# Transposing one more group of attention probabilities on VectorE instead of TensorE

## The chip, the cores and the metric

The kernel runs on one core of one Trainium2 chip. The metric is the device time of one execution in microseconds; the program is launched once and does everything on the chip. A core has five engines with their own instruction streams: TensorE (PE) for matmuls, VectorE (DVE), ScalarE (ACT), GpSimd (POOL) and SyncE (SP), which here issues nearly all DMAs.

## The reference

Attention inside chunks of 64 tokens, and then a two-layer network with a squared ReLU. There are 8 x 576 = 4608 tokens, 8 heads of 64, and the network is 512 to 2048 to 512.

```
scores = scale * q_c @ k_c.T             # per chunk of 64 tokens, per head
attn = exp(scores - max); attn /= attn.sum + 1e-9
x = (attn @ v_c) as 4608 x 512
h = x @ w_in                             # 4608 x 2048
g = s * relu(h)**2 + b
out = g @ w_out                          # 4608 x 512
```

All inputs are float32, and the kernel keeps float32 accuracy in the large products by splitting each operand into a high and a low part and adding three matmuls: high by high, high by low, low by high.

## The kernel before

Tokens come in 36 tiles of 128, and four tiles make a block, so there are nine blocks. Within a block the loop over `j` runs over the 16 slices of the inner dimension 2048: `up(j)` multiplies x by one slice of `w_in` (12 matmuls of 128x512 into `ps_h`), `square(j)` and `bias(j)` turn the result into the two parts `gh` and `gl`, and `down(j - 2)` multiplies these by a slice of `w_out` (12 matmuls into the four `ps_o` tiles). `down` lags two steps behind, so the loop has 18 steps.

The attention of the next block is computed inside the loop of the present one, in two groups of two tiles. `attention_plan` holds a table of places: a place `(j, 0)` is before `up(j)`, `(j, 1)` behind it, and `(j, 2)` between `square(j)` and `bias(j)`. The first group starts at n = 1 and the second at n = 9. For the second group that gives: scores behind up(9), the maximum at (9, 2), the subtraction at (10, 2), exp at (11, 0), the sum at (11, 2), the division (`norm`) before up(13), the transposition of the probabilities, and the product with the values (`values`) behind up(15), whose result is split into the two parts of x (`x_hi` on ScalarE, `x_lo` on VectorE) in the steps 16.

The probabilities `p` are 128 rows (query tokens) by 8 sets of 128 columns. The product with the values needs them transposed, as `pT`. There are two ways in the code. `transposes` and `copies` have TensorE transpose each 128x128 set into the PSUM tile `ps_a` behind up(14) (line L203), and ScalarE copies them to SBUF before up(15) (L217). `turn` has VectorE transpose them from SBUF to SBUF, in 16 instructions that each handle the 32x32 blocks of one position in all 8 sets (L212): four of them between `square(13)` and `bias(13)`, six before up(14), six between `square(14)` and `bias(14)`. Groups of tiles from 8 on use `turn`.

The first block is special, since the weights are prepared in its loop. They arrive as 64-bit numbers and are turned to float32 and split into parts by the class `Pair`, step by step: `scale` and `tail` on ScalarE (L102, L106), `bits` on VectorE (L112, L114), `add` on GpSimd (L120), `hi` on ScalarE (L124), `lo` on VectorE (L128). Pair k holds the `w_in` slice of step k + 1 and the `w_out` slice of step k - 1. In step j VectorE makes `lo` of pair j, which the third matmul of up(j + 1) needs first, and the `bits` of pair j + 2. So up(15) needs the `lo` of pair 14, and down(14) that of pair 15.

The order on each engine is the order of the code; nothing is moved by a scheduler. `square(j)` is L273 on ScalarE and L274 on VectorE, `bias(j)` is L279 on ScalarE and L280 on VectorE, `up` is L266, `down` L291, the scores L172, `values` L225.

Of the kernel before, what the change touches and what calls it, by code (L numbers as in the profile page):

```python
# [19 lines left out]
def local_attention_then_squared_relu_mlp(ctx: ExitStack, tc, qkv, w, s, b, out):  # L20
# [221 lines left out]
    def block(tb0, bank):  # L242
        x = [xp.tile([P, NHP, 4 * P], F32R, name=n) for n in ("xh", "xl")]
        return x, [Attention(tb0 + i, x, i * P, bank) for i in range(0, 4, N)]
# [73 lines left out]
    def attention_plan(tb0):  # L318
        x, groups = block(tb0, steady_bank)
        plan = {}  # L320
        for a, n in zip(groups, (1, 9)):
            for at, *fs in (((n - 1, 0), a.load_qk, a.load_v), ((n, 1), a.scores), ((n, 2), a.peak), ((n + 1, 2), a.sub),
                            ((n + 2, 0), a.exp), ((n + 2, 2), a.sum), ((n + 4, 0), a.norm),
                            ((n + 6, 1), a.values), ((n + 7, 0), a.x_hi), ((n + 7, 2), a.x_lo)):
                plan.setdefault(at, []).extend(fs)

            if a.tb < 8:
                turns = ((n + 5, 1), a.transposes), ((n + 6, 0), a.copies)
            else:
                turns = [(at, partial(a.turn, range(*r))) for at, r in (((n + 4, 2), (0, 4)), ((n + 5, 0), (4, 10)), ((n + 5, 2), (10, 16)))]  # L330
            for at, f in turns:
                plan.setdefault(at, []).append(f)
        return x, plan, plan.pop((0, 0))
# [3 lines left out]
    for a in (one, two):  # L337
        a.p = wp.tile([P, 4, DM], F32, name="wp")[:, 0:2, :].rearrange("p i (g c k) -> p (i g) c k", g=NHP, c=2)
    next_x, plan, (load_next_qk, load_next_v) = attention_plan(4)
    pair = [Pair(k) for k in range(NJ)]  # L340
    one.load_qk()
# [61 lines left out]
    for tb0 in range(0, NTB, 4):  # L403
# [42 lines left out]
        if tb0 + 8 < NTB:  # L446
            next_x, plan, loads = attention_plan(tb0 + 8)
# [33 lines left out]
```

## Time and profile before

| | |
|---|---|
| median of 3 runs | 864.5 us (864.43 to 864.71) |
| profiled execution | 864.6 us, its span 862.8 us |
| granted TensorE clock | 1.000 |
| PE busy | 847.9 us (98%), 5874 matmuls |
| DVE busy | 472.2 us (55%) |
| ACT busy | 295.4 us (34%) |
| POOL busy | 42.1 us (5%) |

The time runs from the start to the end of one execution on the device; the span is from the first to the last instruction in the trace. In the rows shown below a matmul's duration overlaps that of the next one, since matmuls are pipelined; what a matmul costs is read from start to start. In a row of the timeline stand the start, the duration, the engine, the line, the operation, the tile written and those read, the shape and the count; a bracket at the end gives the idle time before it and what ended that. The rows of groups have busy time and mean duration in ns, then the idle time before. The rows of waits have the total, the number and the longest. The first block lasts from about 22 us to 124.7 us.

### The profile page before, as it was taken

How to read it: one execution, taken by the hardware profiler on the slowest of the kernel's cores; microseconds unless marked ns; L12 is line 12 of the kernel's file. 1: busy time of each engine (PE TensorE's matmuls, PEld its weight loads, DVE VectorE, ACT ScalarE, POOL GpSimd, SP SyncE). 2: the span in 40 equal slices, each digit the busy share in tenths (PEclk: the TensorE clock that was granted, in tenths of full speed). 3: DMA queues.
4: the chain of work that ended last, by engine and by line, in shares of the span. 5: the costliest groups of instructions: out<-in, count | busy, mean ns of one | idle time of the engine just before them, and what ended most of it. 6: DMA issues, size and time to landing. Idle time of an engine off the chain costs nothing.

```text
span 862.8 us, 13668 instructions
## 1 busy us (share of the span) xinstructions
PE 847.9 (98%) x5874; PEld 697.2 (81%) x5874; DVE 472.2 (55%) x710; ACT 295.4 (34%) x437; POOL 42.1 (5%) x24
## 2 busy tenths in 40 slices
PE   8899999999999999999999999999999999999998
PEld 7677788888888888888888888888888888888886
DVE  6898945646464646364554556473636464543222
ACT  5777743222322232223222332223222322232222
POOL 2434310000000000000000000000000000000000
PEclk9999999999999999999999999999999999999999
DMA  8646430200210030203020212002020300010001
GB/s 330 232 168 245 149 108 15 74 2 25 98 39 36 2 122 1 74 1 123 0 74 1 73 51 72 4 25 98 3 72 1 123 0 26 1 49 1 1 0 50
DMA packets 20369, 55.41 MB, mean 64 GB/s; under 512 B 2260, under 2 KB 2516, under 8 KB 20308
## 3 DMA queue, kind: packets, MB, share of 16 engines
q1 hardware_dynamic: 20160, 54.40, 18.0%
q8 instruction: 46, 0.75, 0.4%
q10 hardware_dynamic: 148, 0.13, 0.0%
q14 instruction: 15, 0.12, 0.0%
HBM read 45.09 MB, written 9.44 MB: 63 GB/s over the span
## 4 chain that ended last, share of the span: by engine, by line
PE 88%; DVE 7%; issue 2%; ACT 2%; DMA 1%; POOL 0%; SPq 0%; ACTq 0%; POOLq 0%
PE ps_o L291 42%; PE ps_h L266 41%; PE ps_a L225 2%; PE ps_a L172 2%; DVE wp L128 2%; DVE ps_h L274 1%; DVE f L114 1%; DVE f L112 1%; DVE g L280 1%; ACT g L279 1%; DMA raw<-in_w_dram 1%; DVE z L191 0%; PE ps_h L67 0%; DVE m L177 0%; POOL f L120 0%
## 5 line engine op out<-in xcount | busy, mean ns | idle before, releaser
L291 PE MATMUL ps_o<-wp,g 128*128 128x512 f32 x1728 | 415.6, 391 | 0.0
L266 PE MATMUL ps_h<-xh,wp 128*128 128x512 f32 (+1 forms) x1160 | 378.9, 389 | 5.6 <-DVE g L280 3.4
L291 PEld LDWEIGHTS ps_o<-wp,g 128*128 128x128 f32 x1728 | 322.3, 188 | 67.8
L274 DVE SCALAR_TENSOR_TENSOR ps_h<-ps_h,sb,r 128x512 f32<-128x512 f32 x144 | 109.2, 758 | 320.2 <-ACT r L273 319.7
L266 PEld LDWEIGHTS ps_h<-xh,wp 128*128 128x128 f32 x1160 | 216.8, 188 | 53.0 <-DVE wp L128 4.1
L266 PE MATMUL ps_h<-xl,wp 128*128 128x512 f32 (+1 forms) x580 | 224.9, 388 | 0.0
L273 ACT ACTIVATE r<-ps_h 128x512 f32<-128x512 f32 x144 | 85.9, 597 | 366.9 <-PE ps_h L266 366.9
L279 ACT ACTIVATE g<-ps_h,sb 128x512 fp32r<-128x512 f32 x144 | 99.1, 688 | 125.9 <-DVE ps_h L274 125.9
L280 DVE SCALAR_TENSOR_TENSOR g<-ps_h,sb,g 128x512 fp32r<-128x512 f32 x144 | 107.6, 747 | 47.8 <-ACT g L279 46.9
L266 PEld LDWEIGHTS ps_h<-xl,wp 128*128 128x128 f32 x580 | 108.9, 188 | 22.1
L212 DVE STREAM_TRANSPOSE pT<-p 32x256 f32<-32x256 f32 x224 | 97.5, 435 | 3.9
L120 POOL TENSOR_TENSOR f<-f,raw 128x1024 int32<-128x1024 int32 (+1 forms) x17 | 39.5, 2323 | 67.6 <-DVE f L114 48.7
L308 ACT COPY f<-ps_o 128x512 f32<-128x512 f32 (+1 forms) x35 | 20.4, 583 | 41.4 <-PE ps_o L291 39.2
L114 DVE SCALAR_TENSOR_TENSOR f<-raw,f 128x1024 uint32<-128x1024 uint32 (+1 forms) x17 | 21.9, 1286 | 0.5
L102 ACT ACTIVATE f<-raw 128x1024 f32<-128x1024 f32 (+1 forms) x17 | 18.5, 1088 | 10.4 <-DMA raw<-in_w_dram 9.2
L128 DVE TENSOR_TENSOR wp<-f,wp 128x1024 fp32r<-128x1024 f32 (+1 forms) x17 | 22.0, 1294 | 0.0
L240 DVE TENSOR_TENSOR xl<-ps_a,xh 128x512 fp32r<-128x512 f32 x32 | 20.5, 683 | 1.7 <-ACT xh L236 1.7
L196 DVE TENSOR_TENSOR p<-p,z 128x1024 f32<-128x1024 f32 x16 | 19.6, 1226 | 0.6
L172 PEld LDWEIGHTS ps_a<-raw 64*64 64x64 f32 x960 | 15.4, 134 | 5.3 <-issue 5.3
L225 PEld LDWEIGHTS ps_a<-pT,v 64*64 64x64 f32 x960 | 15.4, 134 | 5.3 <-issue 4.9
L124 ACT CAST wp<-f 128x1024 fp32r<-128x1024 f32 (+1 forms) x17 | 16.9, 996 | 7.6 <-POOL f L120 7.5
L177 DVE TENSOR_REDUCE m<-ps_a 128x16 f32<-128x1024 f32 x16 | 19.4, 1215 | 0.0
(45 smaller groups left out, 214.9 us busy)
## 6 DMA issues: line engine op xcount, KB each, us to landing
raw<-in_w_dram SPq DMA_DIRECT2D x32, 512.0 KB, 4.8
raw<-in_qkv_dram SPq DMA_DIRECT2D x30, 512.0 KB, 4.6
out_dram<-f SPq DMA_DIRECT2D x35, 256.0 KB, 2.1
v<-in_qkv_dram SPq DMA_DIRECT2D x30, 256.0 KB, 3.0
wp<-in_qkv_dram SPq DMA_DIRECT2D x6, 512.0 KB, 6.0
wp<-in_qkv_dram SPq DMA_DIRECT2D x6, 256.0 KB, 8.0
out_dram<-f ACTq DMA_DIRECT2D x1, 128.0 KB, 2.1
out_dram<-f SPq DMA_DIRECT2D x1, 128.0 KB, 2.0
```

The costliest lines, as they stand in the source:

```text
L114: nc.vector.scalar_tensor_tensor(out=u, in0=high, scalar=0x80000000, in1=u, op0=ALU.bitwise_and, op1=ALU.bitwise_or)
L120: nc.gpsimd.tensor_tensor(out=i, in0=i, in1=low.bitcast(I32), op=ALU.add)
L128: nc.vector.tensor_tensor(out=lo, in0=f, in1=hi.bitcast(F32), op=ALU.subtract)
L172: nc.tensor.matmul(out=self.ps[cols, c, i * NHP + hp, :], lhsT=qk[rows, 0, h, :], rhs=qk[rows, 1, h, :], start=True, stop=True)
L212: nc.vector.transpose(out=self.pT[k].rearrange("p i a t -> p (i a) t")[:, :, t], in_=p[t, :, k])
L225: nc.tensor.matmul(out=ps[i if apart else 0][cols, c, i * NHP + hp, :], lhsT=self.v[i][rows, h, :], rhs=self.pT[rows, i, hp, cols], start= ...
L266: nc.tensor.matmul(out=self.ps[j][:, cols], lhsT=w[:, c, :], rhs=x[:, c, :], start=(c == 0 and i == 0), stop=(c == NHP - 1 and i == 2))
L273: nc.scalar.activation(out=r, in_=ps, func=AF.Relu)
L274: nc.vector.scalar_tensor_tensor(out=ps, in0=ps, scalar=s_col, in1=r, op0=ALU.mult, op1=ALU.mult)
L279: nc.scalar.activation(out=gh, in_=ps, func=AF.Identity, bias=b_col)
L280: nc.vector.scalar_tensor_tensor(out=gl, in0=ps, scalar=b_col, in1=gh.bitcast(F32), op0=ALU.add, op1=ALU.subtract)
L291: nc.tensor.matmul(out=self.acc[t], lhsT=x[:, ts], rhs=w, start=(j == 0 and i == 0), stop=(j == NJ - 1 and i == 2))
```

## The change

The second group of the second block (tiles 6 and 7) is computed in the loop of the first block. It now takes the way by VectorE, as the groups of tiles 8 to 35 do. The first group of the second block (tiles 4 and 5) and the first block's own groups keep the way by TensorE.

```diff
@@ -324,7 +324,7 @@
                             ((n + 6, 1), a.values), ((n + 7, 0), a.x_hi), ((n + 7, 2), a.x_lo)):
                 plan.setdefault(at, []).extend(fs)
 
-            if a.tb < 8:
+            if a.tb < 6:
                 turns = ((n + 5, 1), a.transposes), ((n + 6, 0), a.copies)
             else:
                 turns = [(at, partial(a.turn, range(*r))) for at, r in (((n + 4, 2), (0, 4)), ((n + 5, 0), (4, 10)), ((n + 5, 2), (10, 16)))]
```

On VectorE, in steps 13 and 14 of the first block (L274 is `square`, L280 `bias`, L128 the low part of a pair of weights; the two L274 are those of steps 13 and 14, the L128 between them is pair 14, the last one pair 15):

```order
 L114 SCALAR_TENSOR_TENSOR f<-raw,f 128x1024
 L274 SCALAR_TENSOR_TENSOR ps_h<-ps_h,sb,r 128x512
-L280 SCALAR_TENSOR_TENSOR g<-ps_h,sb,g 128x512
-L128 TENSOR_TENSOR wp<-f,wp 128x1024
-L274 SCALAR_TENSOR_TENSOR ps_h<-ps_h,sb,r 128x512
+L212 STREAM_TRANSPOSE pT<-p 32x8x32 x4
+L280 SCALAR_TENSOR_TENSOR g<-ps_h,sb,g 128x512
+L212 STREAM_TRANSPOSE pT<-p 32x8x32 x6
+L128 TENSOR_TENSOR wp<-f,wp 128x1024
+L274 SCALAR_TENSOR_TENSOR ps_h<-ps_h,sb,r 128x512
+L212 STREAM_TRANSPOSE pT<-p 32x8x32 x6
 L280 SCALAR_TENSOR_TENSOR g<-ps_h,sb,g 128x512
```

Ten transposes now stand between `square(13)` and the low part of pair 14, and six more between `square(14)` and `bias(14)`.

On TensorE, at the end of up(14) and the beginning of down(12) and up(15):

```order
 L266 MATMUL ps_h<-xl,wp 128x512
 L266 MATMUL ps_h<-xh,wp 128x512
-L203 MATMUL ps_a<-ident,p 128x128 x8
 L291 MATMUL ps_o<-wp,g 128x512 x12
 L266 MATMUL ps_h<-xh,wp 128x512
```

The eight transposes are gone from between up(14) and down(12), and nothing else on TensorE is moved.

Still on TensorE, the waits from up(15) to the values, as they stand in the changed kernel (a name in brackets is the engine whose semaphore the instruction waits for; DMAHW are DMA queues):

```order
L266 MATMUL ps_h<-xh,wp 128x512 [waits DVE_49]
L266 MATMUL ps_h<-xl,wp 128x512
L266 MATMUL ps_h<-xh,wp 128x512 [waits DVE_49]
...
L225 MATMUL ps_a<-pT,v 64x64 [waits DMAHW6_49,PE_49]
L225 MATMUL ps_a<-pT,v 64x64 [waits DVE_49]
L225 MATMUL ps_a<-pT,v 64x64
L225 MATMUL ps_a<-pT,v 64x64 [waits DVE_49]
```

The third matmul of up(15) waits for VectorE's low part, as it did before. The first matmul of the values waited for ScalarE's copies before; now the second and the fourth wait for VectorE's transposes.

## The prediction

> **What bounds the kernel now.** I read the page first: how busy each engine is, and the shares of the chain that ended last.
>
> ```profile
> span 862.8 us, 13668 instructions
> PE 847.9 (98%) x5874; PEld 697.2 (81%) x5874; DVE 472.2 (55%) x710; ACT 295.4 (34%) x437; POOL 42.1 (5%) x24
> PE 88%; DVE 7%; issue 2%; ACT 2%; DMA 1%; POOL 0%; SPq 0%; ACTq 0%; POOLq 0%
> ```
>
> TensorE carries 88% of the chain, so what TensorE is spared is worth its full time, as long as nothing makes TensorE wait. VectorE is busy 55% on average, which suggests room for seven microseconds of transposes. But VectorE also has 7% of the chain, and an average cannot say where. So I read next who TensorE waited for, then its groups from 128 us to the end, and then the busy time around the place of the change.
>
> ```profile
> PE ps_h L266 <- DVE g L280: 3.4, 3, 2.4
> PE ps_h L266 <- DVE wp L128: 2.2, 3, 1.5
> ...
> L291 PE MATMUL ps_o<-wp,g 128*128 128x512 f32 x1536 | 369.2, 391 | 0.0
> L266 PE MATMUL ps_h<-xh,wp 128*128 128x512 f32 x1015 | 332.8, 390 | 0.3 <-DVE g L280 0.3
> ...
> 95.00:106.00 11.00, 11.00 (x49) 8.79 (x47) 10.14 (x13) 8.59 (x11) 4.89 (x2) 1.00 0.42 155
> 106.00:118.00 12.00, 11.68 (x115) 9.61 (x115) 9.01 (x11) 5.73 (x10) 2.43 (x1) 1.00 0.06 11
> ```
>
> The two waits on VectorE are the largest that TensorE has in the whole span. From 128 us on, its groups hold 0.3 us of idle time between them. So TensorE has no idle time after the first block into which a delay could vanish: what the first block loses, the end loses. The last two rows (length, then busy time of PE, PEld, DVE, ACT, POOL) are the stretch that matters. From 95 to 106 us VectorE is busy 10.14 of 11 us, from 106 to 118 us 9.01 of 12. The split of the weights still runs there: the change puts about 7 us into a stretch with about 3 us free.
>
> Now TensorE's timeline at the place: start, duration, line, tile, count.
>
> ```profile
> 106.33 0.73 PE L266 MATMUL ps_h<-xh,wp 128*128 128x512 f32 x2 [0.33 <-DVE wp L128]
> ...
> 108.50 0.39 PE L266 MATMUL ps_h<-xh,wp 128*128 128x512 f32 x1
> 108.73 1.03 PE L203 MATMUL ps_a<-ident,p 128*128 128x128 f32 x8
> 109.53 2.98 PE L291 MATMUL ps_o<-wp,g 128*128 128x512 f32 x12
> ...
> 112.57 0.39 PE L266 MATMUL ps_h<-xl,wp 128*128 128x512 f32 x1
> 112.80 0.62 PE L266 MATMUL ps_h<-xh,wp 128*128 128x512 f32 x2
> ...
> 114.84 0.39 PE L266 MATMUL ps_h<-xh,wp 128*128 128x512 f32 x1
> 115.15 1.16 PE L225 MATMUL ps_a<-pT,v 64*64 64x64 f32 x64
> ```
>
> This is: up(14) to 108.50, the eight transposes, down(12), up(15) from 112.34, the values at 115.15, and behind them down(13) to down(15). The first row is the third matmul of up(14): it takes the low part of its weights, and it stood still until VectorE's L128 (`lo`) had made it. The third matmul of up(15), at 112.80, takes what the next L128 makes. VectorE, with POOL's last add and the two copies on ScalarE that go:
>
> ```profile
> 105.06 1.22 DVE L128 TENSOR_TENSOR wp<-f,wp 128x1024 fp32r<-128x1024 f32 x1
> 106.19 0.69 DVE L112 TENSOR_SCALAR f<-f 128x1024 uint32<-128x1024 uint32 x1
> ...
> 108.06 0.75 DVE L274 SCALAR_TENSOR_TENSOR ps_h<-ps_h,sb,r 128x512 f32<-128x512 f32 x1
> 108.36 2.43 POOL L120 TENSOR_TENSOR f<-f,raw 128x1024 int32<-128x1024 int32 x1 [4.81 <-issue]
> 109.57 0.75 DVE L280 SCALAR_TENSOR_TENSOR g<-ps_h,sb,g 128x512 fp32r<-128x512 f32 x1 [0.76 <-ACT g L279]
> 110.23 1.64 DVE L128 TENSOR_TENSOR wp<-f,wp 128x1024 fp32r<-128x1024 f32 x1
> 112.40 0.76 DVE L274 SCALAR_TENSOR_TENSOR ps_h<-ps_h,sb,r 128x512 f32<-128x512 f32 x1 [0.53 <-ACT r L273]
> ...
> 113.78 1.06 ACT L217 COPY pT<-ps_a 128x512 f32<-128x512 f32 x2
> ...
> 117.33 1.06 ACT L236 CAST xh<-ps_a 128x512 fp32r<-128x512 f32 x2
> 118.43 1.29 DVE L240 TENSOR_TENSOR xl<-ps_a,xh 128x512 fp32r<-128x512 f32 x2 [0.21 <-ACT xh L236]
> ```
>
> The L128 for up(15) runs from 110.23 to 111.87, 0.93 us ahead of the matmul that needs it. That margin is all there is.
>
> **The change part by part.** The removed transposes: without them the first matmul of `down` starts 0.23 us after the last of `up`, as these rows show.
>
> ```profile
> 97.00 0.39 PE L266 MATMUL ps_h<-xh,wp 128*128 128x512 f32 x1
> 97.23 2.88 PE L291 MATMUL ps_o<-wp,g 128*128 128x512 f32 x12
> ```
>
> With them it is 109.53 - 108.50 = 1.03 us. TensorE is spared 0.80 us, and this is the most that the change can give. The two copies on ScalarE (1.06 us) are on no path: up(15) is finished behind them, and the values start at 115.15, 0.31 us after its last matmul.
>
> The sixteen VectorE transposes: in the second block the same code stands between the same operations, and its rows give the spacing.
>
> ```profile
> 151.23 0.76 DVE L274 SCALAR_TENSOR_TENSOR ps_h<-ps_h,sb,r 128x512 f32<-128x512 f32 x1 [1.55 <-ACT r L273]
> 151.90 1.77 DVE L212 STREAM_TRANSPOSE pT<-p 32x256 f32<-32x256 f32 x4
> 153.70 0.75 DVE L280 SCALAR_TENSOR_TENSOR g<-ps_h,sb,g 128x512 fp32r<-128x512 f32 x1
> 154.49 2.69 DVE L212 STREAM_TRANSPOSE pT<-p 32x256 f32<-32x256 f32 x6
> 157.21 0.76 DVE L274 SCALAR_TENSOR_TENSOR ps_h<-ps_h,sb,r 128x512 f32<-128x512 f32 x1
> ```
>
> Start to start: L274 to transposes 0.67, four transposes 1.80, L280 0.79, six transposes 2.72. Laid from L274 at 108.06: four transposes at 108.73, L280 at 110.53 (its input from ScalarE is there at 109.57), six transposes at 111.32, L128 at 114.04. L128 then runs without POOL beside it and takes 1.22 instead of 1.64, so the low part is ready at 115.26. At 106.33 TensorE went on 0.05 us after L128 ended, so the third matmul of up(15) comes at 115.31 instead of 112.80: 2.5 us late. TensorE itself would have been there at 112.00.
>
> The second wait: behind L128 stand L274 at 115.17 (1.13 later, as from 105.06 to what followed it), then the last six transposes, from 115.96 to 118.68. Up to the change the values waited for ScalarE's copies; now their second and fourth matmul wait for these transposes. Up(15) needs 115.15 - 112.80 = 2.35 us from its third matmul to the values, plus about 0.1 for the slower restart (0.73 instead of 0.62 us in the two rows), so TensorE is ready at 117.75 and waits another 1.0 us. The values begin at 118.7 instead of 115.15: 3.55 us late. The two delays are nested. The transposes end at 118.7 in any case, so the values alone would fix this time even if L128 were early.
>
> What stands behind them on VectorE: L280 of j=14 (to about 119.5), L128 of pair 15 (to 120.6), L274 and L280 of j=15 (to about 122.8). down(14) needs the first two at 119.8 + 2.72 = 122.5, and down(15) the last at 125.2, so these are covered by 1.9 and 2.4 us; if that cover went, each further microsecond would count in full. The split of the values into x (1.06 on ScalarE, 1.3 on VectorE) follows, to about 124.3, and next block's up(0) comes at 128. No queue of DMAs is passed or moved, and POOL's work is unchanged.
>
> The sum: +2.5 (low weights late; the 0.80 saved is already in it) + 0.1 (restart) + 1.0 (transposed probabilities late) = +3.55, which I round to +3.5. The profiled execution took 864.6 us (its span of 862.8 and 1.8 around it), 0.1 above the median of 864.5. The forecast is 868.1 us, with 867.7 to 868.5 for this case: 0.2 us either way for the spacing, and 0.2 for the spread of the runs.
>
> What no row shows is a transpose beside POOL's add, which runs until 110.79. Lower bound of its price: nothing, as for this reduction with one input from SBUF, which lies wholly beside an add and takes what it takes elsewhere.
>
> ```profile
> 95.50 2.45 POOL L120 TENSOR_TENSOR f<-f,raw 128x1024 int32<-128x1024 int32 x1 [3.17 <-DVE f L114]
> 95.86 1.21 DVE L191 TENSOR_REDUCE z<-p 128x16 f32<-128x1024 f32 x1
> ...
> L191 DVE TENSOR_REDUCE z<-p 128x16 f32<-128x1024 f32 x2 | 2.4, 1208 | 0.0
> ```
>
> A gain below nothing is excluded, since no row has VectorE faster beside POOL. Upper bound: L128, with two inputs from SBUF, was held 0.42 us while POOL had 0.56 us to go. If the first four transposes were held outright until 110.79, they would start 2.06 us late. I take nothing, since a transpose reads one input like L191.
>
> The Trainium skill's page "SBUF — State Buffer" (SBUF: two separate sides) says that VectorE and GpSimd lock one shared port pair against each other, VectorE when it has two SBUF inputs or runs in a two-port mode. The rows of L128 and L191 agree; by it the sum would stay as it is for a transpose in a one-port mode, and grow by the upper bound in the other.
>
> **The rivals.** Held by POOL: the four transposes wait for the add, and everything behind them is up to 2.06 us later: 870.1 us. For it: L128's 1.64. Against it: L191's 1.21.
>
> TensorE's clock drops in the new wait, which is about 3.2 us long (112.1 to 115.3). The trace knows a slow rate at the start, and a wait of 2.36 us without one:
>
> ```profile
> 1.05 3.78 PE L67 MATMUL ps_h<-f 128*128 128x128 f32 x16 [1.05 <-DVE f L54]
> 9.99 2.94 PE L67 MATMUL ps_h<-f 128*128 128x128 f32 x24
> 38.02 0.50 PE L266 MATMUL ps_h<-xh,wp 128*128 128x512 f32 x1 [2.36 <-DVE g L280]
> ```
>
> That is 236 ns a matmul in the first 3.8 us and 122 ns later, half the rate. If the wait brought this back, the 2.35 us of up(15) would take 4.7 us, the values would start at 120.0 instead of 118.7, and the end would be 869.4 us. Against it: 3.2 us is only a little beyond the 2.36 us that left no mark.
>
> The Trainium skill's page "TensorE: Matmul & The Clock Gate" (Part 1) has the clock fall to half after an idle window of about 3.4 us. By that rule a wait of 3.2 us just escapes, and one lengthened by POOL would not; the trace's 2.36 us agrees, and no run so far shows the edge.
>
> Not slower: VectorE absorbs the transposes. The place is the ten transposes ahead of L128. L128 would end at 111.87 plus their time less up to 0.42 (POOL gone), and TensorE, spared 0.80, would be there at 112.00. They cost nothing up to 0.55 us and break even at 1.35 us, which is 0.135 us each; the last six must also fit ahead of 115. Then it would be 863.8 us, or up to 864.6. Against it: the rows give 0.44 us each, without spread. That the edit does nothing is excluded by the order of the instructions.
>
> **How the numbers follow.** Forecast 0.80; held by POOL 0.06; clock 0.07; not slower 0.07. A measurement here tells about 0.2% (1.7 us) from no change. Since the most to gain is 0.80 us, faster by more than that gets 0.02 and within it 0.05; the other cases are all slower, 0.93. The range 867.4 to 869.6 takes in the forecast with its spread and the clock case; it leaves out 870.1 and the not slower case, 13 in 100.
>
> **What the new profile would show.** Right: L203 only for the first group of the second block and the two of the prologue; ten transposes between L274 and L128 near 108.7 to 114; a wait of about 3.2 us ahead of the third matmul of up(15), put down to DVE L128; a wait of about 1 us ahead of L225, put down to DVE L212; the next blocks unchanged but shifted by 3.5 us. Wrong: L128 ahead of 112, transposes shorter than 0.4 us, a first set of four much longer than 1.8 us, or matmuls at half rate after the wait. If the block that follows had lost time of its own, my claim that only these two waits matter would be wrong.

## The result and the profile after

The changed kernel takes 868.65 us (median of five runs, 868.44 to 871.46) against 864.7 us (864.43 to 866.22): a ratio of 1.0052, 95% interval 1.0041 to 1.0063. It is 4 us slower. The forecast was 868.1, within 867.4 to 869.6. The profiled execution took 868.72 us, with a mean granted clock of 0.996; the profiled one of the kernel before had 1.000. The mean alone says little, since other runs of the kernel before, no longer than this one, have 0.996 to 1.000; what counts is where the clock was low.

VectorE at the place of the change, in the timeline of the changed kernel, with POOL's add beside it:

```profile
108.07 0.75 DVE L274 SCALAR_TENSOR_TENSOR ps_h<-ps_h,sb,r 128x512 f32<-128x512 f32 x1
108.37 2.44 POOL L120 TENSOR_TENSOR f<-f,raw 128x1024 int32<-128x1024 int32 x1 [4.80 <-issue]
108.73 1.77 DVE L212 STREAM_TRANSPOSE pT<-p 32x256 f32<-32x256 f32 x4
110.53 0.75 DVE L280 SCALAR_TENSOR_TENSOR g<-ps_h,sb,g 128x512 fp32r<-128x512 f32 x1
111.32 2.68 DVE L212 STREAM_TRANSPOSE pT<-p 32x256 f32<-32x256 f32 x6
114.03 1.23 DVE L128 TENSOR_TENSOR wp<-f,wp 128x1024 fp32r<-128x1024 f32 x1
115.17 0.75 DVE L274 SCALAR_TENSOR_TENSOR ps_h<-ps_h,sb,r 128x512 f32<-128x512 f32 x1
115.95 2.71 DVE L212 STREAM_TRANSPOSE pT<-p 32x256 f32<-32x256 f32 x6
```

Every start is within 0.02 us of the one that was laid out. The first four transposes lie wholly beside POOL's add and take 1.77 us, what they take in the second block without it. L128, which ran 1.64 us beside the end of that add, now comes later and takes 1.23.

TensorE, same stretch:

```profile
108.51 0.39 PE L266 MATMUL ps_h<-xh,wp 128*128 128x512 f32 x1
108.74 2.88 PE L291 MATMUL ps_o<-wp,g 128*128 128x512 f32 x12
...
111.70 0.39 PE L266 MATMUL ps_h<-xl,wp 128*128 128x512 f32 x1
115.31 1.22 PE L266 MATMUL ps_h<-xh,wp 128*128 128x512 f32 x2 [3.22 <-DVE wp L128]
116.33 0.63 PE L266 MATMUL ps_h<-xl,wp 128*128 128x512 f32 x1
...
118.97 0.40 PE L266 MATMUL ps_h<-xh,wp 128*128 128x512 f32 x1
119.30 1.16 PE L225 MATMUL ps_a<-pT,v 64*64 64x64 f32 x64
```

The transposes are gone and down(12) follows up(14) at once. The third matmul of up(15) waits 3.22 us for L128 and comes at 115.31. Behind the wait a matmul takes 0.63 us instead of 0.39, and from start to start 0.42 instead of 0.23. The values start at 119.30, which is 4.15 us later than before, and they do not wait for the transposes, which ended at 118.66. The two profiled times differ by 4.1 us, so the whole loss is here. The clock, from the view of busy time by stretch (the column before the last two is the granted clock):

```profile
114.00:115.00 1.00, 0.00 (x0) 0.00 (x0) 0.97 (x1) 0.00 (x0) 0.00 (x0) 1.00 0.00 0
115.00:115.30 0.30, 0.00 (x0) 0.00 (x0) 0.30 (x2) 0.00 (x0) 0.00 (x0) 0.74 0.00 0
115.30:118.50 3.20, 3.19 (x8) 2.52 (x9) 3.08 (x7) 0.69 (x1) 0.00 (x0) 0.50 0.00 0
118.50:119.00 0.50, 0.50 (x4) 0.39 (x2) 0.47 (x2) 0.00 (x0) 0.00 (x0) 0.94 0.00 0
```

At the end of the wait the clock falls to half. The rows add up to 0.26 x 0.3 + 0.5 x 3.2 + 0.06 x 0.5 = 1.71 us of lost clock, which at half rate is a stretch of 3.4 us.

So there were three candidate costs: the late low part of the weights, the late transposed probabilities, and the slow clock. The experiments separate them. Of five runs of one kernel one or two are sometimes 1 to 3 us longer, so the lowest value is given beside the median. In a profiled one of these (the repeat of the changed kernel below, 871.71 us) a load of weights landed late, as the two rows of ScalarE below show, first the run of 868.72 us, then this one; up(14) ended 1.69 us later there. Each experiment's time stands beside runs of the kernel before on the same chip (medians 864.59 to 864.66). In some of the experiments' rows the line numbers are up to four higher (`values` is L229 for L225, `up` L270 for L266).

```profile
84.15 1.15 ACT L102 ACTIVATE f<-raw 128x1024 f32<-128x1024 f32 x1 [1.74 <-DMA raw<-in_w_dram]
85.82 1.15 ACT L102 ACTIVATE f<-raw 128x1024 f32<-128x1024 f32 x1 [2.88 <-DMA raw<-in_w_dram]
```

### The profile page after: what moved, and what is told of

Same layout as the page of the kernel before. It is cut to its first block, busy times and chain, and to the rows that moved or that the text cites. A ratio compares the mean times of both kernels' runs of the same rounds, so it can differ in the third digit from the quotient of the medians.

```text
span 866.9 us, 13666 instructions
## 1 busy us (share of the span) xinstructions
PE 850.0 (98%) x5866; PEld 698.4 (81%) x5866; DVE 478.4 (55%) x726; ACT 294.8 (34%) x435; POOL 42.1 (5%) x24
## 4 chain that ended last, share of the span: by engine, by line
PE 87%; DVE 8%; issue 2%; ACT 1%; DMA 1%; POOL 0%; SPq 0%; ACTq 0%; POOLq 0%
PE ps_o L291 42%; PE ps_h L266 41%; PE ps_a L225 2%; DVE wp L128 2%; PE ps_a L172 2%; DVE ps_h L274 1%; DVE f L114 1%; DVE f L112 1%; DVE g L280 1%; ACT g L279 1%; DMA raw<-in_w_dram 1%; DVE pT L212 0%; DVE z L191 0%; PE ps_h L67 0%; DVE m L177 0%
## 5 line engine op out<-in xcount | busy, mean ns | idle before, releaser
L266 PE MATMUL ps_h<-xh,wp 128*128 128x512 f32 (+1 forms) x1160 | 381.0, 391 | 7.6 <-DVE wp L128 4.2
L274 DVE SCALAR_TENSOR_TENSOR ps_h<-ps_h,sb,r 128x512 f32<-128x512 f32 x144 | 109.1, 758 | 319.2 <-ACT r L273 318.7
L266 PEld LDWEIGHTS ps_h<-xh,wp 128*128 128x128 f32 x1160 | 218.1, 189 | 55.4 <-DVE wp L128 6.0
L266 PE MATMUL ps_h<-xl,wp 128*128 128x512 f32 (+1 forms) x580 | 225.8, 389 | 0.0
L280 DVE SCALAR_TENSOR_TENSOR g<-ps_h,sb,g 128x512 fp32r<-128x512 f32 x144 | 107.6, 747 | 46.5 <-ACT g L279 45.5
L266 PEld LDWEIGHTS ps_h<-xl,wp 128*128 128x128 f32 x580 | 109.5, 189 | 22.3
L212 DVE STREAM_TRANSPOSE pT<-p 32x256 f32<-32x256 f32 x240 | 104.5, 435 | 4.1
L128 DVE TENSOR_TENSOR wp<-f,wp 128x1024 fp32r<-128x1024 f32 (+1 forms) x17 | 21.5, 1268 | 0.0
L225 PEld LDWEIGHTS ps_a<-pT,v 64*64 64x64 f32 x960 | 15.4, 134 | 5.3 <-issue 5.3
L182 DVE TENSOR_TENSOR p<-ps_a,m 128x1024 f32<-128x1024 f32 x16 | 19.4, 1215 | 0.0
```

What stands on the lines that cost most here:

```text
L128: nc.vector.tensor_tensor(out=lo, in0=f, in1=hi.bitcast(F32), op=ALU.subtract)
L212: nc.vector.transpose(out=self.pT[k].rearrange("p i a t -> p (i a) t")[:, :, t], in_=p[t, :, k])
L225: nc.tensor.matmul(out=ps[i if apart else 0][cols, c, i * NHP + hp, :], lhsT=self.v[i][rows, h, :], rhs=self.pT[rows, i, hp, cols], start= ...
L266: nc.tensor.matmul(out=self.ps[j][:, cols], lhsT=w[:, c, :], rhs=x[:, c, :], start=(c == 0 and i == 0), stop=(c == NHP - 1 and i == 2))
L274: nc.vector.scalar_tensor_tensor(out=ps, in0=ps, scalar=s_col, in1=r, op0=ALU.mult, op1=ALU.mult)
L280: nc.vector.scalar_tensor_tensor(out=gl, in0=ps, scalar=b_col, in1=gh.bitcast(F32), op0=ALU.add, op1=ALU.subtract)
```

## The experiments

**No transposes.** The most that the change could give.

```diff
+        def fill(self):
+            self.pT = att.tile(...)
+            nc.gpsimd.memset(self.pT, 0.015625)
...
+            elif a.tb == 6:
+                turns = [((n + 3, 0), a.fill)] + [(at, partial(a.turn, range(*r))) for at, r in ()]
```

> The second group of the second block is not transposed at all: GpSimd fills its pT with a constant in step 12, where GpSimd is idle. Left out: that group's transposition. My theory, that TensorE is spared 0.80 us and that the whole loss comes from VectorE's sixteen transposes: 863.8 us, the third matmul of up(15) 0.93 + 0.1 us behind the low part of its weights, with no wait. If the loss had another source in the change (the PSUM bank that is no longer taken, the copies that are gone from ScalarE), it would stay at 868 to 869 us.

Measured: 863.94 us (863.86 to 864.28) against 864.59; ratio 0.9991, interval 0.9982 to 1.0. In its trace up(15) runs without a wait. This settles two things: the loss is VectorE's sixteen instructions and nothing else in the change, and the gain that they were traded for is 0.65 us by the medians (the interval goes from nothing to 1.6 us) and 0.72 us by the trace, close to the 0.80 read from two gaps.

**Only the last six.**

```diff
+                turns = [((n + 3, 0), a.fill)] + [(at, partial(a.turn, range(*r))) for at, r in (((n + 5, 2), (10, 16)), )]
```

> Only the last six transposes are done, between square(14) and bias(14); the ten ahead of the low part of pair 14 are left out (pT is filled with a constant first). Theory of two nested waits: the low part is ready at 111.9 as before the change, there is no wait in up(15) and no drop of the clock, but the six transposes end at about 115.9, so the values start 0.75 us late: 865.3 us. Rival, that only the late low part costs time: 863.8 us. Rival, that the late pT alone costs the whole: about 868.

Measured: 865.42 us (865.23 to 865.7) against 864.59, as the theory of two waits has it. TensorE's timeline in this run:

```profile
112.01 0.72 PE L270 MATMUL ps_h<-xh,wp 128*128 128x512 f32 x2
...
114.53 0.33 PE L229 MATMUL ps_a<-pT,v 64*64 64x64 f32 x2
115.12 0.33 PE L229 MATMUL ps_a<-pT,v 64*64 64x64 f32 x4 [0.27 <-DVE pT L212]
116.04 1.14 PE L229 MATMUL ps_a<-pT,v 64*64 64x64 f32 x58 [0.59 <-DVE pT L212]
```

The wait in up(15) is gone and the second one stands there (0.27 + 0.59 us), at the second and fourth matmul of the values, as the order of the waits said (each matmul of the values is two instructions in the trace).

**Only the first ten.**

```diff
+                turns = [((n + 3, 0), a.fill)] + [(at, partial(a.turn, range(*r))) for at, r in (((n + 4, 2), (0, 4)), ((n + 5, 0), (4, 10)), )]
```

> Only the ten transposes ahead of the low part of pair 14 are done; the last six are left out (pT is filled with a constant first). Theory: the third matmul of up(15) still waits until 115.3 and the clock drops behind the wait, so that up(15) takes until 119 and the values start at 119.3 as in the changed kernel, where they did not wait for the last six: 868.6 us, no change. If the clock holds in this run: values at 117.75, 867.1 us. Rival, that the last six transposes set the time: 864 to 865 us.

Measured: 869.03 us (868.93 to 869.93) against 864.59. Leaving out six of the sixteen transposes gives nothing back. The late low part and the slow clock behind it are enough for the whole loss.

```profile
115.17 1.22 PE L270 MATMUL ps_h<-xh,wp 128*128 128x512 f32 x2 [3.18 <-DVE wp L128]
...
119.17 0.63 PE L270 MATMUL ps_h<-xh,wp 128*128 128x512 f32 x1
119.73 1.74 PE L229 MATMUL ps_a<-pT,v 64*64 64x64 f32 x64
```

In this execution (869.93 us, the longest of the five) the slow stretch lasted longer, 6.8 us by its clock rows, and took in the values too (1.74 instead of 1.16 us).

**Keeping TensorE busy in the wait, first try.**

```diff
+                    if self.tb0 == 0 and j == 15 and c == 0 and i == 1:
+                        dummy = steady_bank(1)
+                        for _ in range(24):
+                            nc.tensor.matmul(out=dummy[:, 0, 0:P], lhsT=ident, rhs=ident, start=True, stop=True)
```

> The changed kernel with 24 idle matmuls of 128x128 (identity by identity, into a PSUM tile that nobody reads) between the second and the third matmul of up(15), about 2.9 us, which TensorE otherwise spends waiting. Theory: the granted clock stays at 1.0, up(15) goes on at 115.3 at full rate and ends at 117.5; now the values do wait, for the last six transposes, until 118.7: 868.0 us, 0.6 less than the changed kernel. Rival, that the drop of the clock costs nothing since the transposes end late anyway: 868.65 us, with the values at 119.3.

Measured: 868.96 us (868.71 to 870.47), not the 868.0 expected. My size was wrong: the 24 matmuls are 48 instructions in the trace and took 5.5 us, longer than the wait, so they cost at least what they saved. What it does show is that up(15) ran at the full clock behind them (granted clock 1.00).

**The same with 11.**

> As the run with 24 idle matmuls, with 11: the 24 took 5.5 us, twice what I meant, since each is two instructions in the trace, so 11 take about 2.5 us of the 3.2 us wait. Theory: TensorE waits another 0.7 us and goes on at 115.3; the clock stays at 1.0; up(15) ends at 117.6; the values wait for the last six transposes until 118.7: 868.0 us. Rival, that the drop costs nothing: 868.65 us, with the values at 119.3.

Measured: 868.42 us (868.0 to 869.77), with two of the five runs above 869.4. On its own this did not tell 868.0 from 868.65, so it was run again beside the changed kernel itself:

> The changed kernel itself, on the same chip as the next two, so that differences of half a microsecond can be read: 868.65 us as before, with one stretch of half clock behind the wait in up(15); where that stretch is twice as long, about 0.5 us more.

> The 11 idle matmuls once more, now beside the changed kernel: if the drop of the clock costs what the trace of the first run said (0.58 us), its median lies 0.4 to 0.7 us below that of the changed kernel. If the drop costs nothing, they are equal within 0.2 us.

Measured on one chip: the changed kernel 868.86 us (868.76 to 871.71), with the idle matmuls 867.96 us (867.81 to 868.07). Eleven useless matmuls make the kernel 0.9 us faster, somewhat more than the 0.4 to 0.7 expected. The interval of the ratio to before is 1.0035 to 1.0062 for the changed kernel and 1.0023 to 1.0048 with the idle matmuls; they overlap, but the lowest of the changed kernel's runs lies 0.7 us above the highest of the others. The timeline with the idle matmuls (L271):

```profile
111.81 2.62 PE L271 MATMUL ps_a<-ident 128*128 128x128 f32 x22
115.18 0.73 PE L266 MATMUL ps_h<-xh,wp 128*128 128x512 f32 x2 [0.76 <-DVE wp L128]
...
117.37 0.40 PE L266 MATMUL ps_h<-xh,wp 128*128 128x512 f32 x1
117.70 0.34 PE L225 MATMUL ps_a<-pT,v 64*64 64x64 f32 x6
118.60 1.14 PE L225 MATMUL ps_a<-pT,v 64*64 64x64 f32 x58 [0.56 <-DVE pT L212]
```

This is the course that the forecast described: the third matmul at 115.2, full rate, then the second wait until 118.6, and 868.0 us. In the profiled execution of the changed kernel's repeat the wait was 3.16 us, and the clock was at half behind it for 6.8 us, twice as long as in the first trace.

**Idle matmuls, and the values moved behind down(13).**

```diff
-                            ((n + 6, 1), a.values), ((n + 7, 0), a.x_hi), ((n + 7, 2), a.x_lo)):
+                            ((n + 7, 0) if a.tb == 6 else (n + 6, 1), a.values), ((n + 7, 0), a.x_hi), ((n + 7, 2), a.x_lo)):
```

> The same 11 idle matmuls, and the values of this group moved from behind up(15) to behind down(13), so that the transposes have 2.7 us more. Theory: only the late low part is left, without the drop of the clock: up(15) goes on at 115.3 instead of 112.8, nothing waits later: 864.6 + 2.5 + 0.1 = 867.2 us. Rival, that the end of the last six transposes sets the time through something other than the values (the low part of pair 15, bias(14)): 868 or more.

Measured: 867.28 us (867.08 to 868.61). With the clock held and the second wait moved out of the way, the late low part alone is left: 867.28 - 864.66 = 2.6 us, the term that the forecast put at 2.5 + 0.1.

**The values moved, without idle matmuls.**

> The values behind down(13), without idle matmuls. Theory: in the changed kernel the slow up(15) hides the wait for the last six transposes, so that moving the values gains nothing by itself: the same as the changed kernel within 0.2 us. Rival, that the last six transposes still hold TensorE: 0.6 to 1.0 us less.

Measured: 869.96 us (868.72 to 871.73), with two of the five runs above 870. The median says nothing; the lowest, 868.72, equals that of the changed kernel beside it, 868.76. The times alone do not settle it, but the trace does (its up(14) ended 1.43 us later than that of the changed kernel, so its rows stand that much later):

```profile
116.74 0.73 PE L266 MATMUL ps_h<-xh,wp 128*128 128x512 f32 x2 [3.21 <-DVE wp L128]
...
120.15 3.49 PE L291 MATMUL ps_o<-wp,g 128*128 128x512 f32 x12
123.57 1.16 PE L225 MATMUL ps_a<-pT,v 64*64 64x64 f32 x64
```

The values wait for nothing, but the slow stretch (granted clock 0.50 from 118 to 121 us) now falls on up(15) and down(13), which takes 3.49 instead of 2.88 us. From the end of up(14) to the next block TensorE needs 20.30 us, against 20.19 in the changed kernel: moving the values alone gains nothing.

**The low part of pair 14 ahead of all sixteen.**

```diff
+            elif a.tb == 6:
+                turns = [(at, partial(a.turn, range(*r))) for at, r in (((n + 5, 3), (0, 10)), ((n + 5, 2), (10, 16)))]
...
                         pair[j].lo()
+                        run(*plan.get((j, 3), ()))
```

> The low part of pair 14 stands ahead of all sixteen transposes: ten between it and square(14), six between square(14) and bias(14). Theory of two nested waits: the low part is ready at 111.9 and up(15) does not wait, but the transposes end at 119.8 (VectorE is held by POOL's add again, and starts ten of them at 111.8), so the values wait about 5.4 us: 869.2 us with the clock at 1.0, and about 870.9 if it drops behind that wait for 3.4 us. Rival, that the order of the low part is the whole loss: 863.8 us.

Measured: 871.46 us (871.03 to 871.57) against 864.66. Mending the wait that the profile names makes the kernel slower by another 2.8 us, since all the transposes now stand behind the low part, and the wait for them is longer than the one that went:

```profile
111.89 0.73 PE L266 MATMUL ps_h<-xh,wp 128*128 128x512 f32 x2
...
114.54 0.30 PE L225 MATMUL ps_a<-pT,v 64*64 64x64 f32 x2
118.91 0.48 PE L225 MATMUL ps_a<-pT,v 64*64 64x64 f32 x4 [4.08 <-DVE pT L212]
119.84 1.96 PE L225 MATMUL ps_a<-pT,v 64*64 64x64 f32 x58 [0.45 <-DVE pT L212]
```

The wait is 4.5 us, and the clock falls behind it too, for longer (same columns as above):

```profile
118.00:118.90 0.90, 0.00 (x0) 0.00 (x0) 0.85 (x3) 0.25 (x1) 0.00 (x0) 0.54 0.00 0
118.90:120.00 1.10, 0.64 (x9) 0.46 (x12) 1.05 (x3) 0.00 (x0) 0.00 (x0) 0.50 0.00 0
120.00:124.00 4.00, 4.00 (x63) 3.43 (x64) 3.12 (x4) 1.60 (x3) 0.00 (x0) 0.50 0.24 67
124.00:125.00 1.00, 1.00 (x4) 0.78 (x3) 0.92 (x2) 0.05 (x1) 0.00 (x0) 0.55 0.77 219
```

Lost clock: 0.46 x 0.9 + 0.5 x 1.1 + 0.5 x 4 + 0.45 = 3.41 us, so 6.8 us at half rate. In its part behind the wait, the last 58 instructions of the values take 0.8 us more than at full rate (to the start of down(13) 1.89 instead of 1.07), and down(13) to down(15) 1.5 us more (9.78 instead of 8.29). These 2.3 us stand in place of the 1.7 in my 870.9, which accounts for the 0.56 us beyond it.

**Repacked.**

```diff
-                            ((n + 6, 1), a.values), ((n + 7, 0), a.x_hi), ((n + 7, 2), a.x_lo)):
+                            *((((17, 0), a.values), ((17, 1), a.x_hi), ((17, 2), a.x_lo)) if a.tb == 6 else
+                              (((n + 6, 1), a.values), ((n + 7, 0), a.x_hi), ((n + 7, 2), a.x_lo)))):
...
+            elif a.tb == 6:
+                turns = [(at, partial(a.turn, range(*r))) for at, r in (((13, 2), (0, 2)), ((14, 3), (2, 3)), ((14, 2), (3, 9)), ((15, 0), (9, 16)))]
...
-                    if j > 1:
+                    if 1 < j < 15:
                         pair[j].lo()
+                        run(*plan.get((j, 3), ()))
...
+                        if j == 14:
+                            pair[15].lo(engine=nc.gpsimd)
```

> A version that should beat both: two transposes in the gap between square(13) and bias(13), then the low part of pair 14 and one more; six between square(14) and bias(14), seven before square(15); the low part of pair 15 made by GpSimd, idle by then; the values behind down(14), the split of x behind them. Theory: the low part of pair 14 is ready at 112.0, when TensorE needs it; the transposes end at 119.7, when down(14) does; small waits of 0.3 us at down(15): 864.0 us against 864.6 before. If the packing fails anywhere, TensorE shows a wait there, and the time is that much higher; the most that it can gain is what the run without transposes showed, 863.9.

Measured: 864.94 us (864.68 to 865.62) against 864.66; ratio 1.0003, interval 0.9994 to 1.0012. The loss is gone, but there is no gain, and the time lies 0.9 us above the expected 864.0. VectorE and TensorE at the end of the first block:

```profile
112.96 2.68 DVE L212 STREAM_TRANSPOSE pT<-p 32x256 f32<-32x256 f32 x6
115.67 0.75 DVE L280 SCALAR_TENSOR_TENSOR g<-ps_h,sb,g 128x512 fp32r<-128x512 f32 x1
116.45 3.16 DVE L212 STREAM_TRANSPOSE pT<-p 32x256 f32<-32x256 f32 x7
119.64 0.76 DVE L274 SCALAR_TENSOR_TENSOR ps_h<-ps_h,sb,r 128x512 f32<-128x512 f32 x1
121.16 0.75 DVE L280 SCALAR_TENSOR_TENSOR g<-ps_h,sb,g 128x512 fp32r<-128x512 f32 x1 [0.76 <-ACT g L279]
...
119.63 1.18 PE L225 MATMUL ps_a<-pT,v 64*64 64x64 f32 x64
121.18 3.34 PE L291 MATMUL ps_o<-wp,g 128*128 128x512 f32 x12 [0.37 <-ACT g L279]
```

VectorE has no gap left until 120.4, and down(15), whose `bias` came last, waits 0.37 us at its start and takes 3.34 instead of 2.88 us. That is about 0.8 us, what the removed transposes had given. So no version of this change that I tried beats the kernel before.

**All traces side by side.** Whether a load lands late before the place no longer matters if only TensorE's time from the last matmul of up(14) to the first of the next block is compared. Before, this is 16.04 us (108.50 to 124.54). The other traces need more by:

| kernel | us more | clock behind the wait |
|---|---|---|
| no transposes | -0.72 | full |
| repacked | 0.06 | full |
| only the last six | 0.81 | full |
| 11 idle matmuls, values moved | 2.62 | full |
| 11 idle matmuls (both traces) | 3.55 | full |
| 24 idle matmuls | 4.50 | full |
| the changed kernel | 4.15 | half for 3.4 us |
| values moved | 4.26 | half for 3.4 us |
| only the first ten | 5.24 | half for 6.8 us |
| the changed kernel, repeat | 5.36 | half for 6.8 us |
| low part first | 7.01 | half for 6.8 us |

With the clock held, the late low part costs 2.62 us and the second wait 0.93 more. The short slow stretch adds 0.60 to these 3.55 and the long one 1.81. The first ten alone cost about the same as all sixteen when both meet the long stretch, so there too the slow matmuls cover the second wait.

## Why the prediction was right

Right, by its steps. The bound: the 55% of VectorE's average said nothing, the stretch from 106 to 118 us said that there was no room, and the run without transposes shows that VectorE's work alone makes the loss. The spacing taken from the second block: every start within 0.02 us. The wait of the third matmul: 115.31 forecast and measured, and worth 2.6 us when isolated, against 2.5 + 0.1. The second wait: forecast until 118.7 and 1.0 us long, measured 118.6 and 0.93 us when it shows (11 idle matmuls, with and without the values moved). The nesting: mending the first wait alone gave nothing back but took 2.8 us more, though the transposes ended later there too. With the clock held, the two waits together cost 3.55 us, the very sum of the forecast. POOL's add does not hold a transpose: lower bound right, and that rival is out. The Trainium skill's page "SBUF — State Buffer" (SBUF: two separate sides) says so for an instruction that neither reads two SBUF operands nor runs in a two-port mode, and this trace agrees with 1.77 us for four beside the add.

Wrong: the step that weighed the clock. I gave it 0.07, on the ground that a wait of 2.36 us had left no mark in the trace of before and that 3.2 us was little more. The slow rows at the start were not a measured drop either: the view of before has a granted clock of 1.00 in them. The clock fell in every trace taken of that order where TensorE stood idle (the changed kernel twice, the first ten alone, the values moved), and with it the second wait vanished from the changed kernel's trace, since the slow matmuls of up(15) ended at 119.3, after the transposes. The term of 1.0 us for the second wait thus became 1.55 us of slow matmuls (119.30 - 117.75). What the clock cost in the end is 0.6 us by the traces (4.15 - 3.55) and 0.9 us by the medians with and without idle matmuls; the difference between the two is not explained. I had put this case at 120.0 for the values and 869.4 us; it was 119.30 and 868.65, since I let the whole of up(15) run slow, while the clock came back at 118.5.

So the number is right in part by luck. Of the signs that the prediction listed, the wait of 1 us ahead of the values did not show, and matmuls at half rate behind the wait, a sign of being wrong, did. The slow matmuls took the place of the second wait and cost only 0.6 us more than it. Where the slow stretch was the long one, as in the profiled execution of the repeat, the same kernel lost 5.36 us; added to 864.6 that would be an estimated 870.0 us, above the range.

The Trainium skill's page "TensorE: Matmul & The Clock Gate" (Part 1) puts the fall behind an idle window of about 3.4 us on a free-running count. The lengths here, 3.4 us and 6.8 us at half clock, fit one and two such windows; but the waits ahead of up(15)'s third matmul were 3.16 to 3.22 us, so an idle stretch of a full window is not needed, and there the measurement decides.

## What to carry to other kernels

An engine's mean occupancy says nothing about the place where work is added: lay the new instructions, with durations from a place where they already run, between the rows that are there, and look at what stands behind them and who waits for it. Where two waits are nested, mending the one that the profile names uncovers the other, and can make things worse. In this kernel every traced wait of 3.2 us that TensorE spent idle was followed by 3.4 or 6.8 us at half clock, so such a wait should be priced with that, and a few useless matmuls in the wait may pay: here 11 of them gave 0.9 us back, while 24 took longer than the wait and gave nothing.

## What the runs showed of the hardware

The clock can fall after less idle time than I had thought. In the changed kernel's trace it also fell early in the first block, when TensorE had waited 2.36 us and had already been going again for about two (columns as above):

```profile
36.00:38.00 2.00, 0.00 (x0) 0.00 (x0) 2.00 (x4) 2.00 (x4) 1.52 (x1) 1.00 1.00 412
38.00:40.00 2.00, 1.58 (x6) 1.01 (x7) 1.97 (x3) 2.00 (x4) 0.00 (x0) 1.00 0.66 207
40.00:42.00 2.00, 2.00 (x7) 1.52 (x5) 2.00 (x3) 0.82 (x2) 0.81 (x1) 0.51 0.82 322
```

In the trace of before, the same wait at the same place left the clock at 1.00. Of the 13 traces, 9 show this early stretch at half clock and 4 do not, and both kinds occur in one and the same kernel (the changed kernel and its repeat). So whether a short wait costs clock differs from run to run. There it cost nothing that the time shows, since TensorE waits for VectorE in the steps that follow: at 57.6 us it goes on in both traces, after a wait of 1.51 us before and of 0.25 us after. In up(15) the short stretch cost 0.6 us and the long one 1.8. The same wait was followed by 3.4 us of it in the changed kernel and by 6.8 in its repeat; why was not tried.
